# FFN1 pairs for gelu in 64x32 tiles: two PSUM banks at once, the row halves exchanged between two turns

## The chip, the cores and the metric

The kernel runs on one core of one Trainium2 chip. The metric is the device time of one execution in microseconds; the time before is 414.62 us, the median of 2 runs (414.05 to 415.18).

## The reference, cut to what matters

```python
x = A_x                                # 1 x 2048 x 448, bf16
xn = layernorm(x)
# branch A: 16 heads of 28, no mask
q, k, v = split(xn @ wqkv)
s = softmax(q k^T * 28**-0.5) v @ wo
# branch B: FFN, 448 -> 1792 -> 448
h = gelu(xn @ w1 + b1)                 # tanh form
f = h @ w2 + b2
return x + s * silu(f)
```

The change touches `xn @ w1 + b1` ahead of gelu, and of that only the tiles that gelu reads straight from PSUM.

## The kernel before, in words

**Tiling.** The 2048 positions are four chunks `c` of 512. The 16 heads are four groups `g` of 4, each head padded from 28 to 32 rows. One block of attention is one group against one chunk; there are 16 blocks, and each has 64 score tiles of 128 keys x 512 queries. TensorE (PE) makes scores by row tiling (mode "row", tiles of 32x128, four heads at once in four PSUM banks), and projections, FFN and P V by column tiling (mode "col", tiles of 128x32, four at once in the four partition quarters of one bank). ScalarE (ACT) takes the exponentials of most score tiles, two or three banks at a time; some groups of four tiles ("late" groups) go to VectorE (DVE) instead, which makes an approximate exponential (L2065). All of PSUM is one ring of eight banks.

**The FFN.** Hidden features are 14 tiles of 128 (`FT`) for each chunk, 56 tiles in all. The contraction over 448 is four k-tiles (`KT`); the fourth has 64 rows of data and, in row 64, a row of ones against the bias. The first 32 tiles (`F0`) are made one by one early on, in gaps (`p_f1`, L1537), and DVE copies them to SBUF before gelu. The other 24 are "directs": 12 pairs (`ND`) which gelu reads from two adjoining PSUM banks. `p_gelu` (L1594) is one stage in the middle of the kernel, between two changes of ACT's function table: it alternates a piece of two or three tiles from SBUF with one pair from PSUM, twelve times, all at L1620. After it FFN2 (`p_f2`, L1632) and the remaining attention blocks follow.

**The pair before.** `p_direct` (L1581) asks the planner for two adjoining banks, then issues bank 0's four k-tiles and bank 1's four k-tiles through `t_f1` (L1569), which calls `_mm` (L125): four matmuls with 128 rows, 32 output columns and 512 positions each. That is 8 tasks of four matmuls for a pair. Pair i may start once pair i-2 is being read by gelu.

**What sets the order.** A greedy planner in the program (`run`, L434) writes each engine's instruction order beforehand. Each process offers one task, with an engine, a duration, a priority (smaller goes first) and, on PE, a mode. Each time the planner takes the engine whose candidate can start first, looks at the candidates of that engine that start within a window `EPS` of it (0.12 us in the block concerned), and puts the one with the smallest rate. The rate is the priority, with a supplement where the mode differs from PE's present one:

```python
def rate(self, t):
    p = t.prio
    if t.E == PE and 1.05 < p < 90 and self.pe_mode != "row" and t.mode != self.pe_mode:
        p += 4 if p > 2 else MP
    return p
```

`start_of` (L207) adds `SWITCH`, 0.1 us, for a change of mode. Pair tasks have priority 3.5; the projections of q and k (`p_q` L1426, `p_k` L1418) have 5 while the gelu stage runs; late groups that go alone (`p_solo`, L1917) have 4.5 there, and with the constants of that block need four free banks at once. While gelu runs, `p_scores` (L1744) holds back the scores of the unit after next until all twelve pairs are read (`dir_read == ND`). The block constants in `BP` change the planner's weights from block to block. On the chip each engine runs its list in order, and waits only on semaphores.

Of the kernel before, what the change touches and what calls it, by code (L numbers as in the profile page):

```python
# [11 lines left out]
PE, ACT, DVE, POOL, SP = ET.PE, ET.Activation, ET.DVE, ET.Pool, ET.SP  # L12
# [8 lines left out]
KT = 4  # L21
T = 16
FT = F // 128
# [67 lines left out]
PIECES, n = [], 0  # L91
for i in range(ND):
    k = F0 // ND + (i < F0 % ND)
# [3 lines left out]
SEM, OWN, SEMW = 0.07, 0.03, 0.15  # L97
# [17 lines left out]
class _Buf:  # L115
    __slots__ = ("w", "r", "tw", "tr")

    def __init__(self):
        self.w = None
        self.r = []  # L120
        self.tw = None
        self.tr = 0.0
# [25 lines left out]
class _Kernel:  # L148
    def __init__(self, nc, A_x, A_wqkv, A_wo, B_w1, B_b1, B_w2, B_b2, out):
        self.nc = nc  # L150
        self.A_x, self.A_wqkv, self.A_wo = A_x, A_wqkv, A_wo
        self.B_w1, self.B_b1, self.B_w2, self.B_b2 = B_w1, B_b1, B_w2, B_b2
        self.out = out
        self.es = ExitStack()
        self.prog = {PE: [], ACT: [], DVE: [], POOL: [], SP: []}
        self.evsem = {}
        self.evcnt = {}
        self.waited = {E: {} for E in self.prog}
        self.tE = {E: 0.9 for E in self.prog}
        self.now = 0.0  # L160
        self.rest_toks = {}
        self.port = {DVE: 0.0, POOL: 0.0}
        self.port_h = None
        self.procs = []
        self.log = []
        self.after = []
        self.n_proc = 0
        self.plan, self.next_m = {}, 0
        self.pe_hist = deque()
        self.pcs, self.bigs, self.smalls, self.hot = {}, [], 0.0, {}  # L170
        self.pe_mode, self.pe_rows, self.pe_start = "full", set(), 0.0
        self.run_toks = set()

    def sem(self, name):
        return self.es.enter_context(self.nc.semaphore(name))
# [30 lines left out]

    def start_of(self, t):  # L207
        s = self.tE[t.E]
        if t.E == PE and t.mode != self.pe_mode:
            s += SWITCH  # L210
        elif t.E == PE and t.mode == "row" and not (t.rows & self.pe_rows):
            s = self.pe_start + 0.01
        if t.port:
            s = max(s, self.port[t.E] + (SEM if t.E == POOL else 0.0))
        if self.pend is not None and t is self.pend["task"]:
            s = max(s, self.pend["t0"])
        own = self.evsem[t.E]
        for b in t.reads:
            if b.tw is None:
                return None  # L220
            s = max(s, b.tw + (OWN if b.w is not None and b.w[0] is own else SEM))
        for b in t.writes:
            mine = b.w is not None and b.w[0] is own
            if not (t.E == PE and mine):
                s = max(s, (b.tw or 0.0) + (OWN if mine else SEM))
            s = max(s, b.tr + (SEMW if t.mode == "row" and t.E == PE else SEM))
        return s

    def put(self, t, start=None):
        if start is None:  # L230
            start = self.start_of(t)
        self.deps(t.E, t.reads, t.writes)
        if t.port and t.E == POOL and start < self.port[POOL] + 4.0:
            self.wait(POOL, self.port_h)
        sem, by = self.evsem[t.E], 1
        if t.tx:
            sem, by = self.s_tx[self.n_tx % len(self.s_tx)], 16
            self.n_tx += 1
            if self.evcnt.get(id(sem), 0):
                self.wait(t.E, (sem, self.evcnt[id(sem)]))  # L240
        key = id(sem) if t.tx else t.E
        self.evcnt[key] = self.evcnt.get(key, 0) + by
        if t.E == PE and t.mode == "row":
            for b in map(id, t.writes):
                if self.rest_toks.get(b) is not None:
                    self.wait(PE, self.rest_toks.pop(b))
                elif b in self.rest_toks:
                    self.rest_toks[b] = (sem, self.evcnt[PE])
        self.prog[t.E].append(lambda eng, f=t.fn, s=sem: f(eng).then_inc(s, by))
        h = (sem, self.evcnt[key])  # L250
        if t.E == PE:
            if t.mode == self.pe_mode == "row" and not (t.rows & self.pe_rows):
                self.pe_rows |= t.rows
            else:
                self.pe_rows = set(t.rows)
            sw = SWITCH if t.mode != self.pe_mode else 0.0
            if t.mode != self.pe_mode:
                self.run_toks = set()
            self.run_toks |= set(map(id, t.writes))
            self.pe_mode, self.pe_start = t.mode, start  # L260
            self.pe_hist.append((start - sw, start + t.dur * t.w))
        if t.port:
            self.port[DVE if t.E == POOL else POOL] = start + t.dur
            if t.E == DVE:
                self.port_h = h
        self.tE[t.E] = max(self.tE[t.E], start + t.dur)
        end = start + t.dur + t.lat
        if t.tx:
            end += 1.5 * any(b1 > start + 0.5 * t.dur for _, b1 in self.bigs)
            self.bigs = self.bigs[-3:] + [(start + 0.5 * t.dur, end)]  # L270
        self.mark(h, t.reads, t.writes, end)
        self.log.append((start, t))
        if self.after and t.E == PE and t.mode == "row":
            self.after[0] += 1
            if self.after[0] == 2:
                f, self.after = self.after[1], []
                f()
        return h
# [1302 lines left out]
    def p_direct(self):  # L1581
        K = self
        yield ("until", lambda: K.gu is not None and K.exp_u >= K.gu - 1)
        for i, (f0, nf) in enumerate(K.directs()):
            K.want = 1
            ids = yield ("banks", lambda: K.exp_u >= K.gu - 1 + i if i < 2 else K.dir_read >= i - 1, 3.5, nf)
            K.want = 0
            K.dir_b.append(ids)
            for n in range(nf):
                for k in range(KT):  # L1590
                    yield K.t_f1((f0 + n) // FT, (f0 + n) % FT, K.ring[:, ids[n], :], K.b_ring[ids[n]], k, 3.5)
            K.dir_n += 1

    def p_gelu(self):  # L1594
        K = self
        yield ("until", lambda: K.gu is not None and K.exp_u >= K.gu and K.n_f1 == len(SBT))
        left = [FT] * C
        hf = K.h[:, :, :].rearrange("p c f -> p (c f)")
        for q, pc in enumerate(PIECES):
            if pc:  # L1600
                f0, n = pc
                src = hf[:, 512 * f0:512 * (f0 + n)]
                rd = []
            else:
                i = K.dir_read
                yield ("until", lambda: K.dir_n > i and K.room_free())
                f0, n = K.directs()[i]
                ids = K.dir_b[i]
                src = K.span(ids)
                rd = [K.b_ring[x] for x in ids]  # L1610
                for f in range(f0, f0 + n):
                    K.hf_free(f // FT, f % FT)
            dst = hf[:, 512 * f0:512 * (f0 + n)]
            if not pc:
                dst = dst.rearrange("p (b n) -> p b n", n=512)
            for f in range(f0, f0 + n):
                left[f // FT] -= 1
            wr = [K.b_hf[f // FT][f % FT] for f in range(f0, f0 + n)]
            wr += [K.b_h[c] for c in range(C) if left[c] == 0 and K.b_h[c].tw is None]
            yield _Task(ACT, lambda eng, dst=dst, src=src: eng.activation(dst, src, ACTF.Gelu_apprx_tanh), rd,  # L1620
                        wr, 0.4267 * n + (0.1 if pc else 0.06) + (1.48 if q == 0 else 0), 0.05, -1)
            if not pc:
                K.dir_read += 1
                K.give(ids)
        K.prog[ACT].append(lambda eng: eng.preload_act_table_set("exp_and_others"))
        K.tE[ACT] += 1.48
        for b in K.b_fsb + K.b_sig:
            b.w = K.b_w1.w
            b.r = list(K.b_w1.r) + [K.b_w1pad.w] + K.b_w1pad.r
        K.gelu_done = True  # L1630
# [940 lines left out]
```

## Time and profile before

| | |
|---|---|
| runs, median | 414.62 us (414.05 to 415.18) |
| span of the profiled execution | 412.4 us |
| TensorE clock granted | 1.00 in all slices |
| busy: ACT | 400.7 us (97%) |
| busy: PE | 395.3 us (96%) |
| busy: DVE | 345.6 us (84%) |
| busy: POOL | 194.7 us (47%) |
| gelu stage, from table load to table load | 224.13 to 251.26 us |

The profiled execution's own time is shown as its span, from its first to its last instruction; what lies around it is the difference to the time of a run, 2.2 us against the median. A line number in the profile is the line of the kernel that recorded the instruction: all column-tiled projections and both FFNs are L128, told apart by their operands (`xnT,w` for FFN1, `xnT,wq` and `xnT,wk` for the projections). In a timeline a row begins with the start and the duration in microseconds; "x16" means that 16 instructions are merged into it, and a bracket tells idle time before it and what ended that.

### The profile page before, as it was taken

To read this page: it belongs to the slowest core of one execution; us is meant where nothing else is said; L and a number is where in the kernel's file an instruction comes from. 1 tells how busy PE (TensorE), PEld (TensorE's weight loads), DVE (VectorE), ACT (ScalarE), POOL (GpSimd) and SP (SyncE) were. 2 spreads that over 40 slices of the span, in tenths; PEclk is the share of its full clock that TensorE was granted. 3 is DMA by queue.
4 is the path that set the end of the run, shared out by engine and by line. 5 is a ranking of instruction groups with operands and counts; after the bars stand their busy time and mean duration, and the time that the engine had idled before them with its cause. 6 is when DMAs were issued, how large, how long until landed. Compare 5 with 4: busy or idle time off the path is not lost.

```text
span 412.4 us, 14687 instructions
## 1 busy us (share of the span) xinstructions
PE 395.3 (96%) x6157; PEld 144.0 (35%) x6157; DVE 345.6 (84%) x596; ACT 400.7 (97%) x409; POOL 194.7 (47%) x221
## 2 busy tenths in 40 slices
PE   6999999999999999999999999999999999999996
PEld 5543232333322233232224443332332223333453
DVE  8958798896679888989898117999998999899976
ACT  6999999999999999999999999999999999999995
POOL 7494656649982563255632411156157014553040
PEclk9999999999999999999999999999999999999999
DMA  8801110001000000100330000220010003200072
GB/s 254 288 4 42 4 31 2 23 12 30 18 3 30 2 28 8 33 2 2 99 105 18 28 3 7 53 54 12 21 24 10 27 8 58 72 3 29 24 140 94
DMA packets 18784, 17.56 MB, mean 43 GB/s; under 512 B 8941, under 2 KB 15421, under 8 KB 18686
## 3 DMA queue, kind: packets, MB, share of 16 engines
q1 hardware_dynamic: 16734, 13.55, 11.1%
q0 software_dynamic: 1008, 2.49, 3.5%
q8 instruction: 49, 0.80, 0.8%
q10 hardware_dynamic: 976, 0.57, 0.5%
q14 instruction: 17, 0.14, 0.1%
HBM read 12.54 MB, written 2.88 MB: 37 GB/s over the span
## 4 chain that ended last, share of the span: by engine, by line
PE 65%; ACT 20%; issue 8%; DVE 5%; POOL 1%; ACTq 0%; DVEq 0%; POOLq 0%
PE ring L128 31%; PE ring L1731 17%; PE ring L2320 14%; ACT P L1785 12%; ACT h L1785 7%; ACT xnT L1785 2%; PE ring L1293 1%; PE ring L1544 1%; DVE x_sb L2065 1%; DVE st L1036 1%; PE ring L1142 1%; DVE h L2065 0%; PE ring L1109 0%; PE ring L1224 0%; POOL h L1095 0%
## 5 line engine op out<-in xcount | busy, mean ns | idle before, releaser
L1785 ACT ACTIVATE P<-ring 128x1024 bf16<-128x1024 f32 (+1 forms) x236 | 249.3, 1162 | 1.1 <-PE ring L2320 0.3
L1731 PE MATMUL ring<-qT,kT 32*128 32x512 bf16 (+2 forms) x1131 | 130.5, 359 | 5.3 <-ACT P L1785 1.6
L1785 ACT ACTIVATE h<-ring 128x1024 bf16<-128x1024 f32 (+1 forms) x79 | 85.8, 1177 | 0.4 <-PE ring L2320 0.3
L1731 PEld LDWEIGHTS ring<-qT,kT 32*128 32x128 bf16 x1131 | 35.6, 91 | 119.9 <-ACT P L1785 60.2
L2065 DVE TENSOR_SCALAR vaug<-ring 128x512 uint16<-128x512 f32 x92 | 61.0, 683 | 5.9 <-PE ring L1731 3.8
L128 PE MATMUL ring<-xnT,w 128*32 128x512 bf16 x864 | 57.6, 381 | 0.4 <-ACT h L1785 0.2
L128 PE MATMUL ring<-w,h 128*32 128x448 bf16 x896 | 55.5, 355 | 0.2 <-DVE x_sb L2065 0.2
L2320 PE MATMUL ring<-P,vaug 128*32 128x512 bf16 (+2 forms) x606 | 53.7, 351 | 0.8 <-ACT xnT L1785 0.7
L2427 POOL TENSOR_TENSOR qT<-x_sb,E_sb 128x512 bf16<-128x512 f32 x15 | 17.7, 1179 | 67.3 <-PE ring L1731 19.0
L2416 POOL TENSOR_TENSOR rc<-rs,mone 128x16 f32<-128x16 bf16 x11 | 32.7, 2971 | 29.5 <-DMA rs<-E_sb 27.9
L1785 ACT ACTIVATE xnT<-ring 128x1024 bf16<-128x1024 f32 (+1 forms) x39 | 43.1, 1132 | 0.6 <-PE ring L1731 0.6
L2065 DVE TENSOR_SCALAR w<-ring 128x512 uint16<-128x512 f32 x52 | 34.6, 685 | 2.7 <-PE ring L1731 2.1
L128 PEld LDWEIGHTS ring<-xnT,w 128*32 128x32 bf16 x864 | 20.3, 96 | 26.3 <-issue 6.1
L128 PEld LDWEIGHTS ring<-w,h 128*32 128x32 bf16 x896 | 17.9, 95 | 22.8 <-issue 14.0
L2320 PE MATMUL ring<-h,vaug 128*32 128x512 bf16 x201 | 23.4, 383 | 0.4 <-ACT P L1785 0.4
L1435 DVE CAST qT<-ring 128x512 bf16<-128x512 f32 x15 | 10.3, 688 | 15.3 <-PE ring L128 15.0
L2065 DVE TENSOR_SCALAR h<-ring 128x512 uint16<-128x512 f32 x28 | 18.7, 684 | 3.8 <-PE ring L1731 3.6
L2320 PEld LDWEIGHTS ring<-P,vaug 128*32 128x32 bf16 x606 | 15.9, 95 | 15.5 <-issue 7.2
L1558 DVE CAST h<-ring 128x512 bf16<-128x512 f32 x24 | 16.4, 687 | 5.0 <-PE ring L128 4.9
L2065 DVE TENSOR_SCALAR x_sb<-ring 128x512 uint16<-128x512 f32 x28 | 18.5, 682 | 2.5 <-PE ring L1731 1.6
L1441 POOL TENSOR_TENSOR qsq<-qT 128x512 bf16<-128x512 bf16 x12 | 12.5, 1039 | 15.5 <-DVE qT L1435 15.5
L128 PE MATMUL ring<-wv,xnT 128*32 128x112 bf16 (+1 forms) x512 | 18.1, 261 | 0.5 <-issue 0.3
(248 smaller groups left out, 644.0 us busy)
## 6 DMA issues: line engine op xcount, KB each, us to landing
x_sb<-recs SPq DMA_DIRECT2D x60, 64.0 KB, 2.0
w<-in_B_w_dram SPq DMA_DIRECT2D x1, 1568.0 KB, 7.5
w<-in_B_w_dram SPq DMA_DIRECT2D x1, 1344.0 KB, 8.3
x_sb<-in_A_x_dram SPq DMA_DIRECT2D x2, 448.0 KB, 6.8
out_dram<-in_A_x_dram SPq DMA_DIRECT2D x2, 448.0 KB, 10.6
out_dram<-h POOLq DMA_DIRECT2D x4, 224.0 KB, 5.9
out_dram<-h SPq DMA_DIRECT2D x7, 112.0 KB, 2.7
xnT<-wq POOLq DMA_DIRECT2D x1, 512.0 KB, 5.4
```

The lines of the kernel that those rows point to most:

```text
L128: ins = eng.matmul(out[q:q + 32, :], w[:, q:q + 32], x, tile_position=(0, q), start=start, stop=stop, skip_group_check=True)
L1036: yield _Task(DVE, lambda eng, i=i, t=t: eng.bn_stats(K.st6[:, i, :], K.x_sb[:, c, t, :]), [K.b_x1t if i == 4 else K.b_x[c] if c else K.b_ ...
L1142: return eng.matmul(bank, w[sl, 3, g * 128:(g + 1) * 128], K.xnT[sl, 3, c * 512:(c + 1) * 512], tile_position=pos, start=False, stop=True, ...
L1435: yield _Task(DVE, lambda eng: eng.tensor_copy(qb, bank), [tok], [qr], 0.7, 0.0, dp)
L1441: yield _Task(POOL, lambda eng: eng.tensor_tensor(qs, qb, qb, ALU.mult), [qr], [tq], 1.1, 0.05, 2, port=True)
L1558: yield _Task(DVE, lambda eng: eng.tensor_copy(dst, bank), [tok], wr, 0.69, 0.0, 2)
L1731: return eng.matmul(dst, K.kT[32 * j:32 * j + 32, g, t * 128:(t + 1) * 128], K.qT[32 * j:32 * j + 32, g, c * 512 + q0:c * 512 + q0 + nq], ...
L1785: return eng.activation(reg[:, i0:i0 + n, :], src, ACTF.Exp, scale=SM_SCALE)
L2065: yield _Task(DVE, lambda eng: eng.tensor_scalar(K.part(u, k).bitcast(dt.uint16), K.like(u, bank), SM_SCALE * LOG2E * 128.0, (127.0 - EXP_ ...
L2320: return eng.matmul(acc[32 * j:32 * j + 32, q0:q0 + nq], w, ap[:, col:col + nq] if len(ap.shape) == 2 else ap[:, col // 128:(col + nq) // ...
L2416: yield _Task(POOL, lambda eng: eng.tensor_tensor(K.rc[:, :], K.rs[:, :], K.mone[:, 0:1].to_broadcast([128, 16]), ALU.pow), [K.b_srs, K.b_ ...
L2427: yield _Task(POOL, lambda eng: eng.tensor_tensor(dst, K.rb, E, ALU.mult), [K.b_rb, tE], [K.b_onT[g][c]], 1.15, 0.05, 1, port=True)
```

## The change

`p_direct` no longer makes one bank after the other. A new task `t_pair` issues eight matmuls with 64 rows and 32 columns: for both banks, all four column quarters, one k-tile. In the first turn bank 0 gets the upper half of the rows (partitions 0 to 63) of every k-tile and bank 1 the lower half (64 to 127); in the second turn the halves are exchanged, and the sums go on accumulating in the same banks. There are 8 tasks of eight matmuls for a pair. Between the turns the first task of the second waits for the last matmul of the first (`K.cross`), so that two row halves do not write one bank at the same time. The tasks have a mode of their own, "half", in the planner. The planned start of the second turn is the planned end of the first plus 0.15 us (`SEMW`), and a planned task is 0.22 us with a latency of 0.17 us.

```diff
     def start_of(self, t):
         s = self.tE[t.E]
+        if t.E == PE and t.mode == "half" and self.cross:
+            s = max(s, self.cross[1])
         if t.E == PE and t.mode != self.pe_mode:
             s += SWITCH
...
         self.deps(t.E, t.reads, t.writes)
+        if t.mode == "half" and self.cross:
+            self.wait(PE, self.cross[0])
+            self.cross = None
...
-            for n in range(nf):
+            for turn in range(2):
+                if turn:
+                    mine = K.b_ring[ids[0]].w
+                    K.cross = mine, K.b_ring[ids[0]].tw + SEMW
                 for k in range(KT):
-                    yield K.t_f1((f0 + n) // FT, (f0 + n) % FT, K.ring[:, ids[n], :], K.b_ring[ids[n]], k, 3.5)
+                    yield K.t_pair(f0, ids, k, turn)
             K.dir_n += 1
+
+    def t_pair(self, f0, ids, k, turn):
+        K = self
+
+        def f(eng):
+            ins = None
+            for n in range(2):
+                h = n ^ turn
+                sl = slice(64 * h, 64 * h + 64)
+                c, ft = (f0 + n) // FT, (f0 + n) % FT
+                for q in range(0, 128, 32):
+                    ins = eng.matmul(K.ring[q:q + 32, ids[n], :], K.w1[sl, k, ft * 128 + q:ft * 128 + q + 32],
+                                     K.xnT[sl, k, c * 512:(c + 1) * 512], tile_position=(64 * h, q),
+                                     start=(k == 0 and turn == 0), stop=(k == KT - 1 and turn == 1), skip_group_check=True)
+            return ins
+        rd = [K.b_w1, K.b_w1pad] + [K.b_xnT[(f0 + n) // FT][k // 2] for n in range(2)]
+        return _Task(PE, f, rd, [K.b_ring[i] for i in ids], 0.22, 0.17, 3.5, mode="half")
```

More of the change, by code (lines that the diff above doesn't have):

```diff
@@ L232, in put @@
         self.deps(t.E, t.reads, t.writes)
+        if t.mode == "half" and self.cross:
+            self.wait(PE, self.cross[0])
+            self.cross = None
         if t.port and t.E == POOL and start < self.port[POOL] + 4.0:
```

## The prediction

> **What bounds the kernel now.** I read the page first, for the engines' shares, then the busy time by stretches, then the timelines of ScalarE (ACT) and TensorE (PE) through the stage that the diff touches.
>
> ```profile
> span 412.4 us, 14687 instructions
> ...
> PE 395.3 (96%) x6157; PEld 144.0 (35%) x6157; DVE 345.6 (84%) x596; ACT 400.7 (97%) x409; POOL 194.7 (47%) x221
> ```
>
> ACT is busy for 97% of the span and PE for 96%, so the average does not say which of them sets the end of a stage. The stage itself does:
>
> ```profile
> core 0: us, PE busy (x) PEld busy (x) DVE busy (x) ACT busy (x) POOL busy (x), PEclk, DMA share, GB/s
> 224.00:252.50 28.50, 27.73 (x510) 13.27 (x502) 9.82 (x16) 28.45 (x27) 7.74 (x5) 1.00 0.04 12
> 252.50:400.00 147.50, 145.42 (x2327) 50.73 (x2319) 137.43 (x223) 146.33 (x144) 53.00 (x48) 1.00 0.16 35
> ```
>
> From 224.0 to 252.5 ACT is idle for 0.05 us (28.50 - 28.45), and in the 147.5 us behind it for 1.2 us. ACT has no slack anywhere, so a hole in ACT is lost for good. DVE is two thirds idle in the stage. The ACT timeline shows how the gelu stage runs:
>
> ```profile
> 223.09 1.02 ACT L1785 ACTIVATE P<-ring 128x1024 bf16<-128x1024 f32 x1
> 224.13 1.28 ACT L1620 ACT_TABLE_LOAD   x1
> 225.43 1.48 ACT L1620 ACTIVATE h<-h 128x1536 bf16<-128x1536 bf16 x1
> 226.81 1.01 ACT L1620 ACTIVATE h<-ring 128x1024 bf16<-128x1024 f32 x1
> 227.72 1.47 ACT L1620 ACTIVATE h<-h 128x1536 bf16<-128x1536 bf16 x1
> 229.09 1.01 ACT L1620 ACTIVATE h<-ring 128x1024 bf16<-128x1024 f32 x1
> ...
> 244.60 1.07 ACT L1620 ACTIVATE h<-ring 128x1024 bf16<-128x1024 f32 x1
> ...
> 250.15 1.10 ACT L1620 ACTIVATE h<-ring 128x1024 bf16<-128x1024 f32 x1
> 251.26 1.28 ACT L1625 ACT_TABLE_LOAD   x1
> 252.56 1.02 ACT L1785 ACTIVATE P<-ring 128x1024 bf16<-128x1024 f32 x1
> ```
>
> Gelu alternates between a piece from SBUF and a pair of PSUM banks. Pair 0 is read at 226.81, pair 1 at 229.09: one pair every 2.28 us. Pair 8 is read at 244.60 and pair 11 at 250.15, so the last three intervals are 1.85 us each. PE does this meanwhile:
>
> ```profile
> 217.87 0.39 PE L2320 MATMUL ring<-x_sb,vs 128*32 128x512 bf16 x4
> 218.19 0.40 PE L1731 MATMUL ring<-qT,kT 32*128 32x512 bf16 x4
> 218.51 0.40 PE L2320 MATMUL ring<-x_sb,vs 128*32 128x512 bf16 x4
> ...
> 219.38 0.51 PE L128 MATMUL ring<-ident,zero 128*32 128x128 bf16 x24
> ...
> 223.19 0.40 PE L2320 MATMUL ring<-x_sb,vs 128*32 128x512 bf16 x4
> 223.41 3.62 PE L128 MATMUL ring<-xnT,w 128*32 128x512 bf16 x64
> 226.87 0.39 PE L128 MATMUL ring<-xnT,wq 128*32 128x512 bf16 x4
> 227.08 1.90 PE L128 MATMUL ring<-xnT,w 128*32 128x512 bf16 x32
> ...
> 246.72 1.90 PE L128 MATMUL ring<-xnT,w 128*32 128x512 bf16 x32
> 248.56 0.39 PE L1731 MATMUL ring<-qT,kT 32*128 32x512 bf16 x4
> ```
>
> Pairs 0 and 1 are made back to back from 223.41 to 226.87: 16 tasks of four matmuls, 3.46 / 16 = 0.216 us each. Pair 0 is therefore complete near 225.3, long before its gelu at 226.81. Only then does PE turn to a projection (wq, 226.87), and from there projections fill the gaps between pairs. Grouped over the stage:
>
> ```profile
> L128 PE MATMUL ring<-xnT,w 128*32 128x512 bf16 x384 | 22.4, 379 | 0.0
> L128 PE MATMUL ring<-xnT,wq 128*32 128x512 bf16 x48 | 3.8, 379 | 0.0
> L128 PE MATMUL ring<-xnT,wk 128*32 128x512 bf16 x32 | 2.4, 379 | 0.0
> ```
>
> The pairs are 384 matmuls, 96 tasks, 96 x 0.216 = 20.7 us. The projections are 80 matmuls, 20 tasks, 4.3 us: the last five of head group 3. The chain that ended last runs along PE here,
>
> ```profile
> 223.59 25.04 PE ring L128 x464
> ```
>
> and 464 is just 384 + 80. But PE ends its last pair near 248.5 and ACT reads it at 250.15: PE has about 1.6 us to spare, ACT 0.05. ACT is the bound, with PE close behind it.
>
> **The change, part by part.** The matmul work itself does not shrink. A pair was 8 tasks of four 128x32 tiles; it becomes 8 tasks (2 turns x 4 k) of eight 64x32 tiles, twice the instructions for the same products.
>
> Price of one half task. No row has this shape, so I bound it. Four tiles run side by side in both shapes that are shown (128*32 at 0.216 us a task, the row-tiled scores at 0.39 us for four at once). Lower end: eight also run side by side, 0.216. Upper end: only four do, 0.432. Issue is no obstacle: one of the 24 zero matmuls above lasts 0.22 us,
>
> ```profile
> L128 PE MATMUL ring<-ident,zero x84: 217/219/230, 71.4 to 398.7; 128*32 128x128 bf16 x84
> ```
>
> so their starts fill 0.51 - 0.22 = 0.29 us, 12 ns apart, and eight per 0.216 us need only 27 ns. I take 0.216, because row and column tiling each run at full width in their own rows and nothing in them is shared.
>
> The Trainium skill (TensorE: Matmul & The Clock Gate, "Measured speedup vs the span model") gives 3.07x for 4 tiles and 10.6x for 16, so packing loses a little as tiles are added. My estimate from that page for 8 tiles is some 8% more per task, 0.233 us; by it the sum below would be about 0.8 us longer. No run here shows eight.
>
> Mode switches. The task of 217.87 is followed by a score task after 0.32 us, and that by the next after 0.32, where 0.216 would do: a change of tile shape costs 0.10 us. The Trainium skill (TensorEngine Tiling, "Key Properties") says that a change of mode drains the array. A full drain of the 0.39 us matmul would make it 0.17 instead of 0.10, and three of them 0.2 us more in the sum; the trace holds against that.
>
> The exchange wait. Before turn 1 PE waits on its own semaphore for turn 0's last matmul. Behind it in PE's queue stand turn 1, the next pair and everything else; ACT waits for the pair.
>
> ```profile
> 255.59 0.40 PE L1731 MATMUL ring<-qT,kT 32*128 32x512 bf16 x4
> 256.04 1.45 ACT L1785 ACTIVATE P<-ring 128x1536 bf16<-128x1536 f32 x1 [0.20 <-PE ring L1731]
> ```
>
> These matmuls end at 255.99 and ACT starts at 256.04, a release of 0.05 us. So the wait costs at least 0.39 - 0.216 + 0.05 = 0.22 us, and with a weight load of some 0.1 us not pulled ahead, 0.32. I take 0.32, the planner's own figure too. A pair with nothing in its gap then takes 8 x 0.216 + 0.32 = 2.05 us against ACT's 2.28: hidden. Over the seven intervals of 2.28 PE gains 1.6 us, over the last four (1.85) it loses 0.8. So these waits cost nothing after pair 0. Without that cover, eleven would be 3.5 us.
>
> What fills the first exchange. This is where I see the loss. The planner gives turn 1 a start 0.32 us off; a column-mode task can start after a switch of 0.10, more than the planner's window (0.12) ahead of it, so it is put first. That task is a wq projection: it has priority 5, was held back by the old pair tasks at 3.5, and is ready. Now PE is in column mode, and the planner's rate adds 4 to any task of another mode: turn 1 stands at 7.5, the next projection task at 5. Each of them wins, and as soon as one projection has its third task out the next may take a bank, until all 20 are done. Before, the same 20 tasks lay in gaps between pairs where ACT had its data already. The order is fixed in PE's program, so the chip follows it:
>
> - 223.41 + 0.10 switch + 4 x 0.216 (turn 0) = 224.37
> - + 0.10 switch + 20 x 0.216 = 228.79
> - + 0.10 switch + 3 x 0.216 to the start of turn 1's last task, + 0.39 to its end, + 0.05 release = 229.98
>
> Pair 0's gelu moves from 226.81 to 229.98: **3.17 us of idle ACT**, since the scores behind gelu are held until all pairs are read. From there the stage keeps its old rhythm; every projection is already done, and pair 1 comes 2.05 us after pair 0, just in time. The five DVE casts and POOL squares of the projections come earlier into idle engines: nothing. No DMA and no queue of SP or POOL is moved past in the stage.
>
> Behind the stage. All later work is planned from another state (which banks are free, which late score groups have passed DVE), with block constants that suit the old one; ACT's 1.2 us of idle in 147.5 leaves little to gain. Lower end: one score group more goes to DVE in the idle stage, 4 tiles of half a 0.91 us activation (226.81 to 227.72), -1.8 us. Upper end: one ACT activation in seven (20 of 144) waits for PE as long as this one,
>
> ```profile
> 284.74 3.77 ACT L1785 ACTIVATE P<-ring 128x1024 bf16<-128x1024 f32 x4 [0.28 <-PE ring L2320]
> ```
>
> 20 x 0.28 = 5.6 us. I take +1.5, between them and nearer to what the trace shows.
>
> **Sum.** 412.4 + 3.17 + 1.5 = 417.1 us of span. The median of the runs, 414.62, lies 2.2 us above the profiled span, and I carry that over: **419.3 us**, own range 416.5 to 422.5.
>
> **Rivals.**
>
> 1. *Eight tiles do not run side by side.* A half task takes 0.432. Then PE is the bound: pair 0 comes 8 x 0.216 = 1.7 us later still, and 11 pairs take 11 x (8 x 0.432 + 0.32) = 41.5 us where ACT's rhythm is 7 x 2.28 + 4 x 1.85 = 23.4, 18.2 more. 419.3 + 19.9 = 439. For it: no row of eight. Against it: both directions of tiling run unhindered alone.
> 2. *Half tasks are a little slower*, 0.25 to 0.27. The 88 tasks of 11 pairs add 88 x 0.044 = 3.9 us at 0.26, less the 0.8 us in hand, plus 0.35 for pair 0: 422.7.
> 3. *The first exchange is filled by score tasks.* (Not slower.) Late score groups wait in a list, at priority 4.5, and beat a projection from half mode. They need four free banks at that moment. If they have them, turn 1 follows at once, since row mode carries no penalty, and the four banks that they hold starve the chain of projections later on. The stall falls to some 0.3 us, and DVE takes up one group early, -1.8 us: with the 1.5 us behind the stage kept, 414.6 + 0.3 - 1.8 + 1.5 = 414.6. For it: DVE idles here. Against it: at 224.4 two banks of the last scores and the one of the accumulator are being read still,
>
> ```profile
> 223.70 0.68 DVE L2402 TENSOR_TENSOR E_sb<-ring,wv 128x512 bf16<-128x512 f32 x1
> 224.30 1.28 DVE L2065 TENSOR_SCALAR vaug<-ring 128x512 uint16<-128x512 f32 x2
> ```
>
> which leaves three of the six that the pair does not hold.
>
> 4. *The plan behind the stage loses much more*: the upper end of 5.6 us, 423.4. For it: saturated engines on both sides of every handoff. Against it: the stage order there is ruled by ACT, whose work is unchanged.
>
> **How the numbers follow.** Forecast 0.56, rival 1 0.10, rival 2 0.07, rival 3 0.12, rival 4 0.15. Two per cent, about what a measurement of this kernel can tell from no change, is 8.3 us: 422.9. Above it lie rival 1, half of rivals 2 and 4 and a sliver of the forecast: 0.10 + 0.04 + 0.08 + 0.02 = 0.24. Faster by 2% needs 406 us, which no case gives: 0.02 for the unknown. The rest, 0.74, is within. The range 413.5 to 427 takes in rivals 2, 3 and 4 and leaves out rival 1 and the ends of 3 and 4.
>
> **What would show it.** Right: a hole of some 3 us in ACT ahead of its second gelu, laid to PE; an unbroken run of about 80 wq/wk matmuls between the two turns of pair 0; pairs at about 2.05 us with no ACT idle after pair 1; the end of gelu near 254.4. Rival 1 would show pairs 3.8 us apart and ACT waiting before every one; rival 2 waits that grow toward the last four pairs; rival 3 a score task in the first exchange; rival 4 many ACT waits of 0.1 to 0.3 us after 256. I am wrong altogether if pair 0's gelu stays near 227 and the total still moves by more than 2 us.

## The result and the profile after

The changed kernel takes **427.61 us** (427.48 to 427.74, 2 runs) against 414.62 us: a ratio of 1.032 with a 95% interval of 1.028 to 1.036, slower by 13.0 us. The forecast was 419.3 us with a range up to 427.0; it has the sign right and about a third of the loss. The profiled execution took 427.74 us, and its page begins

```profile
span 425.9 us, 15600 instructions
...
PE 396.3 (93%) x6622; PEld 145.0 (34%) x6622; DVE 343.3 (81%) x593; ACT 403.4 (95%) x411; POOL 195.8 (46%) x222
```

The span grew by 13.5 us, PE's busy time by 1.0 and ACT's by 2.7. PE's loss is nearly all idle time, and ACT's is idle time in the main, so the question is where both engines wait. The loss can be cut at the end of gelu. ACT's timeline of the stage:

```profile
224.09 1.28 ACT L1646 ACT_TABLE_LOAD   x1
...
230.02 1.02 ACT L1646 ACTIVATE h<-ring 128x1024 bf16<-128x1024 f32 x1 [3.15 <-PE ring L1613]
...
232.31 1.01 ACT L1646 ACTIVATE h<-ring 128x1024 bf16<-128x1024 f32 x1
...
254.57 1.28 ACT L1651 ACT_TABLE_LOAD   x1
```

Pair 0 is read at 230.02 where it was 226.81, after 3.15 us of idle ACT laid to PE; no pair behind it is waited for by more than 0.1 us, and the stage ends at 254.57 where it ended at 251.26: **+3.3 us**. The stretches behind it, with columns as before (stretch and its length, then busy time of PE, PEld, DVE, ACT, POOL, clock, DMA share, GB/s), first of after:

```profile
252.50:400.00 147.50, 138.03 (x2190) 48.90 (x2166) 122.97 (x200) 141.28 (x136) 49.24 (x43) 1.00 0.13 30
...
255.80:425.90 170.10, 152.65 (x2638) 57.54 (x2630) 135.70 (x226) 156.21 (x154) 54.57 (x50) 0.99 0.19 41
```

and of before from the same point of the program, the end of the table load, to its end:

```profile
252.50:412.40 159.90, 154.05 (x2579) 55.52 (x2571) 146.34 (x243) 153.82 (x152) 54.03 (x49) 1.00 0.18 41
```

The same stretch takes 170.1 us instead of 159.9: **+10.2 us**, of which 2.4 is more ACT work (156.21 - 153.82) and 7.8 is more ACT idle (13.89 - 6.08). DVE has 10.6 us less to do there, but most of that had moved ahead into the gelu stage; over the whole program DVE makes 244 exponential tiles where it made 248, and ACT makes the four others. From 252.5 to 400 us ACT was idle for 1.2 us before and is now for 6.2. The larger of these idle times in ACT's timeline:

```profile
263.97 1.94 ACT L1811 ACTIVATE P<-ring 128x1024 bf16<-128x1024 f32 x2 [0.64 <-PE ring L2346]
...
267.49 1.45 ACT L1811 ACTIVATE xnT<-ring 128x1536 bf16<-128x1536 f32 x1 [1.58 <-PE ring L2346]
...
355.85 7.31 ACT L1811 ACTIVATE P<-ring 128x1536 bf16<-128x1536 f32 x6 [1.70 <-PE ring L2346]
...
367.36 6.39 ACT L1811 ACTIVATE P<-ring 128x1536 bf16<-128x1536 f32 x5 [1.50 <-PE ring L2346]
...
416.85 1.02 ACT L1811 ACTIVATE P<-ring 128x1024 bf16<-128x1024 f32 x1 [1.47 <-PE ring L1757]
...
423.15 0.54 ACT L2491 ACTIVATE h<-ring 128x448 bf16<-128x448 f32 x1 [2.58 <-PE ring L128]
```

The kernel before has two waits in its tail too, of which the second is at the place of the 2.58:

```profile
407.81 0.54 ACT L2454 ACTIVATE h<-ring 128x448 bf16<-128x448 f32 x1 [1.05 <-PE ring L128]
409.35 0.54 ACT L2465 ACTIVATE h<-ring 128x448 bf16<-128x448 f32 x1 [0.99 <-PE ring L128]
```

Four of the waits in after, 5.4 us, are laid to L2346, the P V products. PE's timeline ahead of the second, and a line of DVE's groups over the whole program, show why:

```profile
263.22 0.61 PE L2346 MATMUL ring<-P,vaug 128*32 128x512 bf16 x7
...
265.17 0.39 PE L2346 MATMUL ring<-wk,vs 128*32 128x512 bf16 x4
...
266.14 0.61 PE L1757 MATMUL ring<-qT,kT 32*128 32x512 bf16 x7
266.68 0.61 PE L2346 MATMUL ring<-xnT,vaug 128*32 128x512 bf16 x5
```

```profile
L2091 DVE TENSOR_SCALAR wk<-ring 128x512 uint16<-128x512 f32 x4 | 2.6, 681 | 0.0
```

From 263.22 to 266.14 PE makes P V products without a break, and no new scores. After the first eight they belong nearly all to late groups, whose probabilities DVE wrote into buffers that had come free, `wk` among them. The products of ACT's own groups stand behind this run, at 266.68, and read `xnT`, the name that ACT writes next, at 267.49: by the trace ACT's wait ended with a P V product that frees such a buffer, not with a score. Nothing there belongs to the edited function.

### The profile page after: what moved, and what is told of

Its sections match the earlier page's. It is cut to its first block, busy times and chain, and to the rows that moved or that the text cites. A ratio compares the mean times of both kernels' runs of the same rounds, so it can differ in the third digit from the quotient of the medians.

```text
span 425.9 us, 15600 instructions
## 1 busy us (share of the span) xinstructions
PE 396.3 (93%) x6622; PEld 145.0 (34%) x6622; DVE 343.3 (81%) x593; ACT 403.4 (95%) x411; POOL 195.8 (46%) x222
## 4 chain that ended last, share of the span: by engine, by line
PE 57%; ACT 22%; issue 9%; DVE 7%; POOL 3%; DVEq 0%; ACTq 0%; POOLq 0%
PE ring L128 22%; PE ring L1757 15%; ACT P L1811 14%; PE ring L2346 13%; ACT h L1811 6%; PE ring L1613 6%; ACT xnT L1811 2%; DVE vaug L2091 2%; DVE x_sb L2091 1%; PE ring L1550 1%; POOL h L1101 1%; DVE st L1042 1%; PE ring L1148 1%; DVE h L2091 0%; PE ring L1115 0%
## 5 line engine op out<-in xcount | busy, mean ns | idle before, releaser
L1757 PE MATMUL ring<-qT,kT 32*128 32x512 bf16 (+2 forms) x1132 | 128.5, 358 | 12.0 <-ACT P L1811 5.1
L2346 PE MATMUL ring<-P,vaug 128*32 128x512 bf16 (+2 forms) x609 | 53.8, 351 | 1.0 <-DVE w L1673 0.3
L128 PE MATMUL ring<-w,h 128*32 128x448 bf16 x896 | 52.6, 355 | 0.3 <-DVE vaug L2091 0.2
L1811 ACT ACTIVATE xnT<-ring 128x1024 bf16<-128x1024 f32 (+2 forms) x40 | 43.2, 1131 | 2.1 <-PE ring L2346 1.6
L128 PE MATMUL ring<-xnT,w 128*32 128x512 bf16 x480 | 35.2, 383 | 0.4 <-ACT h L1811 0.2
L128 PEld LDWEIGHTS ring<-w,h 128*32 128x32 bf16 x896 | 19.1, 96 | 22.8 <-issue 10.6
L2091 DVE TENSOR_SCALAR x_sb<-ring 128x512 uint16<-128x512 f32 x36 | 23.9, 682 | 2.5 <-PE ring L1757 1.6
L1613 PE MATMUL ring<-xnT,w 64*32 64x512 bf16 x768 | 23.5, 378 | 0.8
L2346 PE MATMUL ring<-h,vaug 128*32 128x512 bf16 x197 | 23.1, 383 | 0.4 <-ACT P L1811 0.4
L2346 PEld LDWEIGHTS ring<-P,vaug 128*32 128x32 bf16 x609 | 15.7, 95 | 16.4 <-issue 6.9
L2091 DVE TENSOR_SCALAR h<-ring 128x512 uint16<-128x512 f32 x24 | 16.0, 686 | 3.7 <-PE ring L1757 3.5
L128 PE MATMUL ring<-xnT,wk 128*32 128x512 bf16 x232 | 17.6, 383 | 0.0
L1673 DVE TENSOR_TENSOR w<-ring,wv 128x448 bf16<-128x448 f32 x16 | 9.9, 619 | 9.6 <-PE ring L128 9.6
```

The lines of the kernel that those rows point to most:

```text
L128: ins = eng.matmul(out[q:q + 32, :], w[:, q:q + 32], x, tile_position=(0, q), start=start, stop=stop, skip_group_check=True)
L1613: ins = eng.matmul(K.ring[q:q + 32, ids[n], :], K.w1[sl, k, ft * 128 + q:ft * 128 + q + 32], K.xnT[sl, k, c * 512:(c + 1) * 512], tile_pos ...
L1673: yield _Task(DVE, lambda eng: eng.tensor_tensor(fb, ps, K.b2b, ALU.add), [tok, K.b_b2], [K.b_fsb[c % 2]], 0.63, 0.0, 2)
L1757: return eng.matmul(dst, K.kT[32 * j:32 * j + 32, g, t * 128:(t + 1) * 128], K.qT[32 * j:32 * j + 32, g, c * 512 + q0:c * 512 + q0 + nq], ...
L1811: return eng.activation(reg[:, i0:i0 + n, :], src, ACTF.Exp, scale=SM_SCALE)
L2091: yield _Task(DVE, lambda eng: eng.tensor_scalar(K.part(u, k).bitcast(dt.uint16), K.like(u, bank), SM_SCALE * LOG2E * 128.0, (127.0 - EXP_ ...
```

## The experiments

Two theories. **The tiles**: half tiles and the wait between the turns cost PE time, and the loss spreads from there. **The order**: the planner, given other durations, another mode and a planned wait, writes another order for the whole rest of the program, and that order is worse whatever the tiles are. Each experiment ran with the kernel before on the same chip; a ratio is to that.

**1. Half tiles in the order of before.** The planner sees the old tasks; only what PE is given to do differs: `halves` makes eight half tiles of turn n, and the wait before turn 1.

```diff
+                    t = K.t_f1((f0 + n) // FT, (f0 + n) % FT, K.ring[:, ids[n], :], K.b_ring[ids[n]], k, 3.5)
+                    t.fn, t.pre = K.halves(f0, ids, k, n)
+                    yield t
```

> The instruction order of every engine is that of the kernel before; only the 96 pair tasks are made of 64x32 tiles with the exchange wait. Theory order (the loss comes from the order that the planner writes once the mode 'half' exists, the tiles themselves are free): 12 waits of about 0.29 us and nine gaps with two more mode switches of 0.10 us add 5.3 us to PE between 223.4 and 248.5, of which 1.6 us are in hand, so the end moves by 3 to 4 us: 417.5 to 418.7, ACT idle in the last pairs, and nothing more lost behind the stage. Rival tiles (eight tiles with twice the instructions disturb PE or what follows): 425 or more.

420.08 us (419.70 to 420.67), ratio 1.014 [1.013, 1.016]: +6.0 us, between what the two theories gave this run: 1.4 to 2.6 us above the one, 5 below the other. ACT's timeline, and PE's where the pairs end:

```profile
249.98 1.02 ACT L1647 ACTIVATE h<-ring 128x1024 bf16<-128x1024 f32 x1 [0.93 <-PE ring L1609]
...
255.51 1.28 ACT L1652 ACT_TABLE_LOAD   x1
...
260.17 1.02 ACT L1812 ACTIVATE xnT<-ring 128x1024 bf16<-128x1024 f32 x1 [0.87 <-PE ring L1758]
```

```profile
254.27 0.39 PE L1758 MATMUL ring<-qT,kT 32*128 32x512 bf16 x4
```

PE's first score behind the pairs starts at 254.27 where it was 248.56: 5.7 us late, close to twelve exchanges of 0.29 us and some twenty switches of 0.11 between pairs and the projections that still lie between them. Gelu ends 4.25 us late, so 1.5 of the 5.7 were in hand there, as forecast; but ACT then waits 0.87 us at 260.17 and 0.56 us soon after, where it waited 0.20 before, though nothing more was expected to be lost there, and this execution ends 5.4 us late (a span of 417.8). In this order most of the 1.6 us that PE had in hand at the end of gelu was its lead for the next scores, not slack.

**2. Full-height tiles in the order of after.** Each task of the new order makes one bank with full rows, without a wait.

```diff
-            self.wait(PE, self.cross[0])
...
+            c, ft = (f0 + turn) // FT, (f0 + turn) % FT
+            return _mm(eng, K.ring[:, ids[turn], :], K.w1[:, k, ft * 128:(ft + 1) * 128],
+                       K.xnT[:, k, c * 512:(c + 1) * 512], k == 0, k > 0)
```

> The order of the changed kernel, but each pair task is four matmuls with all 128 rows for one bank, without the exchange wait. Theory order: the hole ahead of the first pair's gelu stays (2.9 us instead of 3.15, the mode switches are gone) and so does what is lost behind the stage: 426.8 to 427.6. Rival tiles: the loss behind the stage goes, 417 to 419.

428.54 us (426.68 to 429.27), ratio 1.034 [1.031, 1.036]: as slow as the whole change. The profiled execution is the fastest, 426.68 at a mean clock of 1.000; the three others, at 0.992 to 0.995, lie above the expected range. Its ACT timeline has the same waits in the same places, each laid to PE:

```profile
229.79 1.02 ACT L1638 ACTIVATE h<-ring 128x1024 bf16<-128x1024 f32 x1 [2.77 <-PE ring L128]
...
254.27 1.28 ACT L1643 ACT_TABLE_LOAD   x1
...
267.19 1.45 ACT L1803 ACTIVATE xnT<-ring 128x1536 bf16<-128x1536 f32 x1 [1.58 <-PE ring L2338]
...
355.55 7.31 ACT L1803 ACTIVATE P<-ring 128x1536 bf16<-128x1536 f32 x6 [1.70 <-PE ring L2338]
```

The order alone makes the loss. In this order the half tiles cost some 1 us at most by the profiled executions (spans of 424.9 and 425.9, with 0.4 of it in the hole), since all projections have been done in the first exchange and the later exchange waits lie in ACT's shadow. Runs 1 and 2 do not add up: the same tiles cost 6 us in an order that packs PE and 1 at most in one that starves ACT.

**3. No penalty between half and column mode in the planner's rate.** After, otherwise.

```diff
-        if t.E == PE and 1.05 < p < 90 and self.pe_mode != "row" and t.mode != self.pe_mode:
+        if t.E == PE and 1.05 < p < 90 and self.pe_mode != "row" and t.mode != self.pe_mode and not {t.mode, self.pe_mode} <= {"half", "col"}:
```

> The changed kernel with one edit: the planner's rate adds nothing between the modes half and col, so no chain of projections is put between the two turns of the first pair. The hole ahead of the first pair's gelu goes and gelu ends near 251.5 instead of 254.6. If the loss behind the stage follows from the hole (everything shifted by 3 us): 415 to 417. Theory state (any other order through the stage hands the later blocks a state that their constants were not chosen for): still 423 to 427.

424.78 us (424.62 to 426.49), ratio 1.026 [1.024, 1.029]. ACT's timeline:

```profile
225.55 1.28 ACT L1646 ACT_TABLE_LOAD   x1
...
252.70 1.28 ACT L1651 ACT_TABLE_LOAD   x1
...
285.19 6.52 ACT L1811 ACTIVATE P<-ring 128x1024 bf16<-128x1024 f32 x7 [1.79 <-PE ring L2346]
```

The stage takes 27.15 us, as before (27.13): the penalty of 4 did fill the first exchange with projections. Yet 10.7 us of loss stay, behind the stage and in new places. This order does not compute the layer, though: the output of run 3 holds values that are not numbers, and why is not known. Its trace shows where ACT waits in that order; the 10.7 us are not the price of a kernel that could be used.

**4. Before, with a pair's task planned at 0.22 us instead of 0.216.** The tiles, waits and modes are those of before; only what the planner makes of them may differ.

```diff
-                    yield K.t_f1((f0 + n) // FT, (f0 + n) % FT, K.ring[:, ids[n], :], K.b_ring[ids[n]], k, 3.5)
+                    t = K.t_f1((f0 + n) // FT, (f0 + n) % FT, K.ring[:, ids[n], :], K.b_ring[ids[n]], k, 3.5)
+                    t.dur = 0.22
+                    yield t
```

> The kernel before with a single number changed in the planner: a pair task is planned with 0.22 us instead of 0.216. Tiles, waits and modes are those of before; only the written order can differ. Theory state: 419 to 424, lost behind the stage as ACT idle and in the tail, gelu ending at 251.3 as before. If the loss needs the changed tiles or the hole: 414.6, no change.

422.40 us (420.92 to 423.78), ratio 1.020 [1.017, 1.022]: **+8.3 us for 4 ns in a plan**, part of it the granted clock: the executions had a mean clock of 0.991 to 0.998, those of before 0.999 to 1.000, and the one at 0.998 took 420.92 us, 6.9 us more. ACT's timeline, and one line of its stretches:

```profile
251.35 1.28 ACT L1627 ACT_TABLE_LOAD   x1
...
256.27 4.62 ACT L1787 ACTIVATE P<-ring 128x1536 bf16<-128x1536 f32 x4 [1.26 <-PE ring L1733]
...
263.21 6.39 ACT L1787 ACTIVATE P<-ring 128x1024 bf16<-128x1024 f32 x5 [0.71 <-PE ring L2322]
...
270.73 4.62 ACT L1787 ACTIVATE P<-ring 128x1536 bf16<-128x1536 f32 x4 [1.13 <-PE ring L2322]
```

```profile
250.00:270.00 20.00, 17.88 (x262) 6.50 (x264) 13.06 (x22) 17.45 (x15) 2.54 (x3) 0.91 0.29 55
```

Gelu ends 0.09 us later than before, so the loss lies behind it. The first wait, 1.26 us, is not the order's alone: the clock was 0.57 from 252 to 256 us. The others stand at a clock of 1.00. The written order also moved work: ACT makes 784 exponential tiles where it made 776, DVE 240 where it made 248, and ACT's busy time behind gelu grew by 3.0 us (158.08 against 155.06).

**5. The hole alone.** Before, with ACT kept busy for 3.6 us ahead of pair 0's gelu by three extra in-place copies; the order is otherwise unchanged.

```diff
+            if q == 1:
+                for w in (1536, 1536, 384):
+                    K.raw(ACT, lambda eng, w=w: eng.activation(hf[:, 0:w], hf[:, 0:w], ACTF.Copy), [], K.b_hf[0][0:3])
```

> The kernel before, with three extra ACT instructions (copies of the first gelu piece onto itself, 1536, 1536 and 384 columns, some 3.2 us) ahead of the first pair's gelu; every engine's written order and every tile stay. This prices the hole by itself. If ACT is the bound and a hole there is lost once and no more: gelu ends 3.2 us later and the whole is 3.0 to 3.4 us longer, 417.1 to 417.5, with no new ACT waits behind the stage. If a shift of 3 us by itself upsets the handoffs of the later blocks: 420 or more.

418.06 us (417.76 to 419.63), ratio 1.009 [1.007, 1.011]: +3.45 us. ACT's timeline (this execution was the 419.63):

```profile
230.51 1.00 ACT L1623 ACTIVATE h<-ring 128x1024 bf16<-128x1024 f32 x1
...
254.96 1.28 ACT L1628 ACT_TABLE_LOAD   x1
...
408.40 1.02 ACT L1788 ACTIVATE xnT<-ring 128x1024 bf16<-128x1024 f32 x1 [1.71 <-PE ring L1734]
```

Pair 0 is read 3.70 us late, 0.11 of which the stage had at its start, and gelu ends 3.70 us late. The three other executions end 3.15 to 3.6 us late: a hole in ACT is lost once, and is neither made good nor grows. The execution with the profile lost 1.7 us more behind the stage, at the wait of 408.40, where before waits 0.35; its clock had been 0.59 from 232 to 236, and what made this wait is not shown.

**6. Another harmless number.** Before, with the first gelu piece planned 0.1 us longer: does the 8 us hang on the pair's task, or on any change of the plan?

```diff
-                        wr, 0.4267 * n + (0.1 if pc else 0.06) + (1.48 if q == 0 else 0), 0.05, -1)
+                        wr, 0.4267 * n + (0.1 if pc else 0.06) + (1.58 if q == 0 else 0), 0.05, -1)
```

> The kernel before with one other number of the planner changed: the first gelu piece is planned 0.1 us longer. Tiles, waits, modes and the stage's order as before, only what is planned behind the stage can differ. Theory state: 418 to 422, lost as ACT waits behind 256. If the first such test was a chance hit and the plan is normally robust: 414 to 415.

421.81 us (419.91 to 425.02), ratio 1.018 [1.013, 1.023]: +7.2 us; the execution at a clock of 0.999 took 419.91, 5.3 us more. Here ACT makes 776 exponential tiles as before, and there are waits like this one in its timeline:

```profile
297.29 4.69 ACT L1785 ACTIVATE P<-ring 128x1024 bf16<-128x1024 f32 x5 [2.21 <-PE ring L2320]
```

**7. After, with other block constants.** The planner ranks its tasks by a row of constants for each block of the program; here the rows of blocks 10 to 16, those behind gelu, are replaced by rows chosen for the new state. The tiles and the edited code stay.

```diff
-    (4, 1, 1, 0.491, 9, 0.12, 1.675, 0.011, 0.163, 1.176, 0.806, 12, 3, 0.03, 4, 4, 0.112, 1, 7, 12, 10, 0.77, 0.757, 50, 25, 0, 0, 4.944, 4, 0, 4.0, 33, 2.325),
+    (4, 1, 2, 0.175, 10, 0.125, 1.601, 0.053, 0.199, 1.049, 0.922, 6, 2, 0.096, 4, 4, 0.097, 2, 6, 9, 11, 0.654, 0.988, 51, 22, 0, 0, 3.378, 4, 0, 3.823, 30, 4.526),
...
```

> The changed kernel with other constants in the planner's table for blocks 10 to 16 alone, chosen anew for the state that the changed stage hands over; the stage, its hole of 3.15 us and the half tiles stay. Theory state: the loss is a matter of constants that do not fit, so a good part of it comes back, 421 to 423, with gelu still ending at 254.6. If the loss is fixed by what the stage leaves behind (later banks, one late group less): no better than 426.

421.25 us (420.96 to 422.26), ratio 1.017 [1.015, 1.018]: half of the loss is gone. In ACT's timeline the wait of block 9 is still there,

```profile
268.22 1.45 ACT L1811 ACTIVATE xnT<-ring 128x1536 bf16<-128x1536 f32 x1 [1.58 <-PE ring L2346]
```

and those at 355.85 and 367.36 are gone.

**8. After, with one late group at a time.** If runs of P V products make the holes, offering the planner one late score group's products instead of all should remove them.

```diff
-            yield from self.pv_task(q, late, ms)
+            yield from self.pv_task(q, late if end else late[:1], ms)
```

> The changed kernel with one edit: at most one waiting late score group is put ahead of a P V task in the middle of a block, instead of all that are ready. If the ACT hole at 267 comes from the three late groups that ran in the exchanges and are all spent in one run of P V ahead of the tasks that free the probability slots, that hole (1.6 us) goes, and those near 356 and 367 with it if they are of the same kind: 423.5 to 425. If it comes from FFN2 crowding PE: holes stay, 427.

423.41 us (423.28 to 424.60), ratio 1.022 [1.020, 1.024], 4.2 us below after's 427.61. The three waits of 1.5 us and more laid to P V products are gone (4.8 us); the first, at 264.00, stays. So does the tail, with waits of 1.70 and 2.83, and five new waits of 0.2 to 0.6 us, 1.8 in all, are the price; the largest of each in ACT's timeline:

```profile
331.48 3.77 ACT L1811 ACTIVATE P<-ring 128x1024 bf16<-128x1024 f32 x4 [0.60 <-PE ring L2346]
...
418.81 0.54 ACT L2491 ACTIVATE h<-ring 128x448 bf16<-128x448 f32 x1 [2.83 <-PE ring L128]
```

**9. Run 8 with other rows for blocks 9 to 16.** If the loss behind gelu is one of order alone, it can be brought to nothing with the half tiles in place, and only the hole should remain. The diff is that of run 8 and eight rows in the manner of run 7.

> The kernel of e8 (changed kernel, one late group at a time) with other planner constants for blocks 9 to 16, chosen anew for the state behind the changed stage. The hole ahead of the first pair's gelu stays, some 3.3 us. Theory state: what was lost behind the stage is all a matter of constants, so only the hole remains, 417.3 to 418.5. If some of it belongs to the change itself (more PE work, a late group less, the later tail): 420 or more.

417.29 us (416.83 to 419.32, 7 runs), ratio 1.006 [1.003, 1.008]: +2.6 us. ACT's timeline, with the one wait of more than 0.23 us between the start of gelu and the tail, and the stretch behind gelu:

```profile
232.94 1.02 ACT L1646 ACTIVATE h<-ring 128x1024 bf16<-128x1024 f32 x1 [3.32 <-PE ring L1613]
...
255.47 1.28 ACT L1651 ACT_TABLE_LOAD   x1
```

```profile
255.50:414.90 159.40, 154.28 (x2543) 55.19 (x2531) 136.06 (x229) 154.33 (x156) 60.00 (x54) 1.00 0.21 44
```

This stretch begins with the table load and holds 159.4 us; before's, from its table load at 251.26 to 412.4, holds 161.1. The whole 10.2 us behind gelu are recovered, and 1.7 more; what is left is the hole of 3.3 us, now at the second pair, and 0.9 us of smaller delays in and ahead of the stage (gelu ends 4.2 us later than in before). It is the best form of the change found, and still behind the kernel before. No run shows whether rows chosen anew would have gained the kernel before something too.

**10. The rows of run 9 on the kernel before.** Are they better rows, or rows for another state?

> The kernel before with the constants for blocks 9 to 16 of e9, its stage and tiles untouched. Theory state: a set of constants is good for one state only, so here the same set costs several us: 420 to 424. If the new set is simply a better one: 411 to 414.

422.02 us (421.32 to 422.94), ratio 1.018 [1.014, 1.021]: +7.3 us. ACT's timeline has a wait that neither kernel had:

```profile
283.05 1.02 ACT L1785 ACTIVATE P<-ring 128x1024 bf16<-128x1024 f32 x1 [2.51 <-PE ring L2320]
```

ACT makes 788 exponential tiles here where it made 776. At a clock of 0.998 the run took 421.35 us, 6.6 us more. The rows that suit the one kernel thus cost the other several us, as the old rows do in after. Run 9's other edit, one late group at a time, is not in run 10, so the rows are tested here without the edit that they were chosen with.

## Why the prediction was wrong, point by point

**Half tasks: right.** The weight loads of the last pairs, in PEld's timeline, where a bracket is the idle time at the exchange:

```profile
246.04 1.43 PEld L1613 LDWEIGHTS ring<-xnT,w 64*32 64x32 bf16 x64 [0.59 <-PE ring L1613]
248.06 1.43 PEld L1613 LDWEIGHTS ring<-xnT,w 64*32 64x32 bf16 x64 [0.60 <-PE ring L1613]
...
252.12 0.56 PEld L1613 LDWEIGHTS ring<-xnT,w 64*32 64x32 bf16 x32 [0.60 <-PE ring L1613]
```

64 loads last 1.43 us and 32 last 0.56, so four tasks take 0.87, 0.217 us each: eight tiles do run side by side, and rivals 1 and 2 are out. The estimate of 0.233 us from the Trainium skill (TensorE: Matmul & The Clock Gate, "Measured speedup vs the span model") is not borne out in a steady stream.

**The exchange wait: right, slightly high.** Pairs start 2.02 to 2.03 us apart; less 8 x 0.217 that leaves 0.29 us for the wait, inside the bounds of 0.22 and 0.32. That it is hidden behind ACT holds in this order, where no pair after the first is waited for by more than 0.1 us. It is not true of the tiles as such: run 1 shows what the prediction called the price "without that cover", and more.

**The first exchange: right, to 0.04 us.** PE's timeline:

```profile
223.14 0.40 PE L2346 MATMUL ring<-x_sb,vs 128*32 128x512 bf16 x4
223.47 1.06 PE L1613 MATMUL ring<-xnT,w 64*32 64x512 bf16 x32
224.46 1.05 PE L128 MATMUL ring<-xnT,wq 128*32 128x512 bf16 x16
...
228.89 1.92 PE L1613 MATMUL ring<-xnT,w 64*32 64x512 bf16 x64
230.74 0.39 PE L1757 MATMUL ring<-qT,kT 32*128 32x512 bf16 x4
```

Turn 0 ends at 224.46, five groups of 16 projection matmuls follow, and turn 1 starts at 228.89; pair 0 is read at 230.02, forecast 229.98, and gelu ends at 254.57, forecast near 254.4. The switch from 223.14 to 223.47 costs 0.33 - 0.216 = 0.11 us. The Trainium skill (TensorEngine Tiling, "Key Properties") states that a change of mode drains the array; the trace agrees that a change costs time, and has less of it than the 0.17 that the prediction worked out for a full drain. Not forecast: later exchanges took score tasks, the first at 230.74; they lie in ACT's shadow. Runs 3 and 5 confirm both ends of this step: without the penalty the hole is gone, and a hole of 3.6 us costs 3.15 to 3.6.

**Behind the stage: this step failed.** The prediction put it as "Upper end: one ACT activation in seven (20 of 144) waits for PE as long as this one", 5.6 us, and "I take +1.5, between them and nearer to what the trace shows". It measured **10.2 us**, nearly twice the upper end; with it in place of 1.5 the sum comes to 428.0, against 427.61. The mechanism was named ("planned from another state"), in the forecast and as rival 4, but its size was taken from the one wait of 0.28 us that the old order shows. That row says what a wait costs in an order without starved stretches. In another order the waits are few and long: 0.64, 1.58, 1.70 and 1.50 us laid to P V products, 1.47 and 2.58 in the tail, where before has 0.99 for the second. And ACT has 2.4 us more work there, with one score group that was DVE's, where the lower end had put one more on DVE. Rival 4's sign, many waits of 0.1 to 0.3 us, was therefore wrong too. Its argument against itself, that "the stage order there is ruled by ACT, whose work is unchanged", fails on both counts: PE's fixed order decides which scores exist when ACT is free, and ACT's share of the exponentials is the planner's choice.

What the order costs when it is written again for a slightly different plan can be read from runs 4, 6 and 10 on the kernel before: 8.3, 7.2 and 7.3 us by the medians, 6.9, 5.3 and 6.6 in the executions with a clock of 0.998 or more. With those in place of 1.5 the forecast would have been 423.1 to 424.7, nearer and still short. How much of the 10.2 us is due to which difference in state (free banks, late groups, mode) was not separated further.

**PE's time in hand: half right.** "PE has about 1.6 us to spare" is true until gelu ends (run 1: 1.5) and wrong beyond it in that run: the lead is used up on the first scores. In after the first score behind the pairs comes 1.46 us ahead of the end of gelu (253.11 against 254.57) where it was 2.70 ahead. It did no harm to the forecast there: ACT does not wait until 263.97, and run 2, with a lead of 2.67, has the same waits.

## What to carry to other kernels

Where a planner writes a fixed order for saturated engines, an edit is to be priced in two parts: what the chip does differently, and what a new order costs by itself; the second is measured by a change of the plan that leaves the tiles and waits as they were (4 ns in one planned duration cost 7 to 8 us here). What is measured so holds more than waiting: the new order may also move work between engines. Compare a new building block inside the old order, and the old block inside the new order, before judging the block: here the half tiles cost 6.0 us in the one and 1 at most in the other. And an engine's lead at the end of a stage is slack only if the next stage does not need it.

## What was not expected of the hardware

In four of the twelve profiles (runs 3 to 6) the granted clock falls to about half in mid-run for 3 to 4 us, each time behind a pause of PE. In run 6's profile, in the stretches view:

```profile
214.00:218.00 4.00, 2.75 (x32) 0.85 (x33) 3.98 (x7) 4.00 (x6) 0.21 (x1) 0.91 0.25 78
218.00:222.00 4.00, 4.00 (x68) 1.44 (x64) 2.06 (x4) 3.07 (x5) 2.30 (x2) 0.67 0.00 1
```

PE was busy for 2.75 of the four microseconds up to 218. Then the clock was 0.67 for 4 us, PE counts as busy all through because its matmuls last longer, and the gelu stage of that execution began 1.3 us late. In run 4 PE waited 0.51 and 1.34 us ahead of 251.47, and the clock was 0.57 from 252 to 256; in run 5 it waited 2.05 us ahead of 231.57, and the clock was 0.59 from 232 to 236. A pause does not always bring this: the kernel before has the same 2.75 us of PE work from 214 to 218, and its clock stays at 1.00. What decides is not shown.

Executions of one kernel go with the mean clock by and large: run 2 took 426.68 us at 1.000 and 428.41 to 429.27 at 0.992 to 0.995. Some half a per cent between executions of a saturated kernel can thus come from the clock, and a profile of one execution can carry a microsecond that the others do not have. An order that makes PE pause may meet such drops more often; that is not shown either.
